# A new beginning for a talking-heads attention kernel: identity first, wider rows, a first chunk of nine tiles, six more score buffers, w_in later

## The chip, the cores and the metric

The kernel runs on one core of a Trainium2 chip. The metric is the device time of one execution in microseconds (us); "before" is the median of three runs. Engines: PE (matmul), DVE (vector), ACT (activation), POOL (GpSimd), SP (here only a queue that issues DMAs).

## The reference

```python
# q, k, v: (4 batches, 12 heads, 448 rows, 64), fp32
scores = scale * np.matmul(q, k.transpose(0, 1, 3, 2))
scores = np.einsum('bhij,hg->bgij', scores, w_pre)       # mixes the heads before the softmax
attn = exp(scores - max); attn = attn / (sum + 1e-09)
attn = np.einsum('bhij,hg->bgij', attn, w_post)          # and after it
x = np.matmul(attn, v)                                   # -> (4, 448, 768)
h = np.maximum(x @ w_in, 0.0)                            # 768 -> 1024
conv_out = sum over 3 taps of conv_w along the rows
out = (h * sigmoid(conv_out)) @ w_out                    # 1024 -> 768
```

The w_in, conv_w and w_out arrays are float64 and are turned to float32 in the kernel, piece by piece ("decode", five short steps on ACT, POOL and DVE).

## The kernel before

A **tile** is ten query rows of a batch with all twelve heads; its 120 lines (10 rows x 12 heads) and four lines of zeros lie on 124 partitions, so that one matmul by a block matrix of w_pre mixes the heads. A **chunk** is 12, 12, 12 or 9 tiles, four chunks to a batch, 16 in all (the table TILES). A chunk goes through these steps:

- `load_q`, `tr_q` / `load_k`, `tr_k`: queries of the chunk and keys of the batch, loaded and transposed. For the first chunks, `load_q0`, `load_k0` load rows as they lie and `tr_q0`, `tr_k0` transpose them on PE by an identity, `out_q0`, `out_k0` copy the result from PSUM. Later ones are transposed on DVE (L553, L569).
- `qk` (L588): scores of two heads at a time, four matmuls; `qk_out` (ACT L443, in chunks 0 and 1 every other one DVE L445) copies them to a buffer `st`, and `relayout` (L604, SP) moves that buffer into `mt`, one of two chunk buffers, where heads and rows share the partitions. There are three `st` buffers; for chunk 0 there is room for all twelve heads. A fourth score waits until the first relayout has landed.
- per pair of tiles: `premix` (L624; L617 where a tile is alone), `row_max` (DVE L629), `row_exp` (ACT L637), `sum_eps` (POOL), `sum_rec`, `post_w` (DVE L655), `postmix` (PE L668), `post_out` (ACT and DVE). The first premix of a chunk needs all twelve relayouts.
- per chunk: `av` (L709), `av_out`.

When a batch is through, `mm1` (L757) multiplies it by w_in, eight column blocks f, two in each chunk of the next batch; after the last chunk come the last batch's mm1 and the gated product with w_out (L851). w_in comes in 24 pieces (`dec_load`, L738), w_out in 24 more.

All instructions stand in an order found ahead of time by `plan`: each operation has a due time, in units of tiles, from a table of numbers P, a cost, and what it must wait for; a small model of the engines puts them in a row, and each engine runs its row in that order. Waits among engines are real semaphores, so an instruction whose input is late holds all that stand behind it on its engine.

The start is written out by hand: `load_weights` (POOL), `prepare` (zeros, the clearing of four partitions of both `mt` by POOL, L492, then the identity), twelve loads of keys and two of queries, `warm_up`, `emit_weights` (the block matrices of w_pre and w_post), and eight matmuls on zeros (`keep_busy`, L512).

Of the kernel before, what the change touches and what calls it, by code (L numbers as in the profile page):

```python
# [25 lines left out]
R, HR = 10, 5  # L26
TILES = (12, 12, 12, 9)
# [7 lines left out]
for _b in range(B):  # L35
    _i = 0
    for _t in TILES:
# [108 lines left out]

QUARTERS = [(hh, dh) for hh in range(2) for dh in range(2)]


def plan(P):  # L150
# [12 lines left out]
    for c in range(2):  # L163
        for g in range(2):
            n = -9 + g if c == 0 else P["q1p"] + .3 * g
            if c:
                add(n + P["q1l"], "SP", (.5, 10, .3), "load_q0", 1, g, after=[("load_q0", 1, g - 1)])
            add(n, "PE", .4, "tr_q0", c, g, after=[("load_q0", c, g)] + (
                [("tr_k0", 5)] + [("out_q0", 0, 0)] * g if c else []))
            add(n, ("DVE", "ACT")[g], .4, "out_q0", c, g, after=[("tr_q0", c, g), ("out_q0", c, g - 1)])  # L170
# [18 lines left out]

    for c in range(NCH):  # L190
        b, i0, T = CHUNKS[c]
        moved = [("relayout", c, h) for h in range(H)]
        for k, some in enumerate(PAIRS[c]):
# [4 lines left out]
            add(n + P["pm"], "PE", .78, "premix", *x,  # L198
                after=moved + free_m + ([("out_q0", 1, g) for g in range(2)] if at < 4 else []))
# [14 lines left out]
            for i in range(len(some)):  # L214
                add(n + 1 + P["po"] + .01 * i, "PE", .5, "postmix", *x, i, after=[("post_w", *x)] + (
# [65 lines left out]
    for i in range(N_PIECES):  # L281
# [6 lines left out]
        add(n - 4, "SP", (.45, 16, .85), "dec_load", i,  # L288
# [8 lines left out]
    for b in range(B):  # L297
        ready = [("av_out", 4 * b + 3, p) for p in (0, 3)] + [("dec_step", i, 4) for i in range(N_IN)]
        for f in range(FC):
            if b + 1 < B:  # L300
                n = BASE[4 * (b + 1) + f // 2] + P["m1"] + P["m1w"] * (f % 2)
                turn = [before["mm1", b, f]]
# [4 lines left out]
            for kk in range(KC):  # L307
                add(n + d * kk, "PE", .77, "mm1", b, f, kk, after=ready + turn + [("mm1", b, f, kk - 1)])
# [54 lines left out]
    for g in range(2):  # L363
        od.done["load_q0", 0, g] = 2.8 + 1.05 * g, "SP"
# [548 lines left out]
```

## Time and profile before

| | us |
|---|---|
| median of 3 runs | 710.15 (708.75 to 711.02) |
| profiled execution, device time | 710.14 |
| its span in the trace | 708.4 |
| PE busy | 663.8 (94% of the span) |
| DVE / ACT / POOL busy | 415.6 / 343.8 / 81.3 |
| DMA | 104.54 MB, mean 148 GB/s |

The span runs from the first to the last instruction on the core; the device time is 1.74 us longer. An engine's busy share is a mean over stages: the start, batch 0 without FFN work, batches 1 to 3 with it, and the end. PE's busy time comes from modelled ends of pipelined matmuls, and a matmul at the lower granted clock lasts twice as long and counts as busy all the same. A DMA share can go over 1, since packets in flight on an engine overlap.

### The profile page before, as it was taken

The numbers are of one execution on the slowest core, as the hardware profiler recorded it, in microseconds if no ns is written. First come the engines' busy times: TensorE is split into PE (matmuls) and PEld (weight loads), VectorE is DVE, ScalarE is ACT, GpSimd is POOL, SyncE is SP. The second block draws the span as 40 slices with busy tenths as digits, with TensorE's granted clock in tenths as the row PEclk, the third lists the DMA queues.
The fourth block names the chain that finished last, engine by engine and source line by source line (L and its number), as shares of the span: only waits on it lengthen the run. The fifth ranks groups of instructions, "written<-read, shape, count | busy, mean of one in ns | idle before, by whom it ended". The sixth has DMA issues, their size and how long they took to land.

```text
span 708.4 us, 23470 instructions
## 1 busy us (share of the span) xinstructions
PE 663.8 (94%) x9876; PEld 421.5 (59%) x9876; DVE 415.6 (59%) x976; ACT 343.8 (49%) x807; POOL 81.3 (11%) x185
## 2 busy tenths in 40 slices
PE   4687789798999999999999999999999999999997
PEld 3244434355474556555555646464565559999997
DVE  3365758776464647455665646454665499998000
ACT  1354637566464556656555755555554354434000
POOL 8010122222100001011001101101001000000000
PEclk7889979999999999999999999999999999999999
DMA  6577877878755467567746565542414344432111
GB/s 110 169 166 179 186 194 206 198 195 191 172 174 158 128 169 185 168 160 207 169 143 165 157 167 153 156 143 96 154 57 149 122 143 127 123 124 83 52 61 44
DMA packets 96005, 104.54 MB, mean 148 GB/s; under 512 B 40872, under 2 KB 84764, under 8 KB 95900
## 3 DMA queue, kind: packets, MB, share of 16 engines
q1 hardware_dynamic: 93997, 102.43, 53.8%
q8 instruction: 77, 1.26, 0.8%
q10 hardware_dynamic: 1807, 0.61, 0.4%
q14 instruction: 28, 0.23, 0.1%
q0 software_dynamic: 96, 0.01, 0.0%
HBM read 48.32 MB, written 15.99 MB: 91 GB/s over the span
## 4 chain that ended last, share of the span: by engine, by line
PE 75%; DMA 14%; DVE 3%; ACT 3%; POOL 2%; issue 1%; SPq 1%; ACTq 0%; DVEq 0%; POOLq 0%
PE h L757 20%; PE o L851 16%; PE s L588 12%; PE a L709 9%; PE t L668 9%; DMA mt<-st 9%; PE m L624 8%; DMA nq<-in_q_dram 2%; DMA raw<-in_moe_w_in_dram 2%; POOL mt L492 1%; DVE nm L629 1%; DMA raw<-in_moe_w_out_dram 1%; ACT st L443 1%; DMA wo<-w_out_s 1%; ACT e L637 1%
## 5 line engine op out<-in xcount | busy, mean ns | idle before, releaser
L757 PE MATMUL h<-x,wi 128*128 128x448 f32 x384 | 156.9, 552 | 0.9 <-DVE x L717 0.9
L588 PE MATMUL s<-mk,mq 64*64 64x448 f32 (+2 forms) x768 | 137.7, 572 | 9.6 <-ACT st L443 8.1
L637 ACT ACTIVATE e<-m,nm 124x448 f32<-124x448 f32 x180 | 114.7, 637 | 64.0 <-DVE nm L629 32.2
L443 ACT COPY st<-s 120x448 f32<-120x448 f32 (+1 forms) x180 | 92.4, 533 | 103.6 <-DMA mt<-st 42.6
L668 PEld LDWEIGHTS t<-wn,e 60*64 60x64 f32 x5760 | 104.0, 136 | 53.7 <-issue 33.2
L629 DVE TENSOR_REDUCE nm<-m 124x1 f32<-124x448 f32 x180 | 106.3, 614 | 50.3 <-PE m L624 50.1
L668 PE MATMUL t<-wn,e 60*64 60x60 f32 x5760 | 110.7, 221 | 9.3 <-DVE wn L655 4.3
L851 PE MATMUL o<-wo,g 128*128 128x384 f32 x672 | 117.4, 337 | 0.0
L851 PEld LDWEIGHTS o<-wo,g 128*128 128x128 f32 x672 | 116.9, 188 | 0.4 <-DVE g L836 0.2
L757 PEld LDWEIGHTS h<-x,wi 128*128 128x128 f32 x384 | 69.3, 190 | 75.5 <-issue 63.1
L624 PE MATMUL m<-mt,wpre 64*64 64x448 f32 (+1 forms) x704 | 102.1, 563 | 7.2 <-DMA mt<-st 3.9
L445 DVE COPY at<-t 128x480 f32<-128x480 f32 (+1 forms) x92 | 61.2, 665 | 55.3 <-PE t L668 55.1
L709 PEld LDWEIGHTS a<-at,v 128*64 128x64 f32 x1536 | 74.3, 137 | 20.8 <-issue 6.4
L709 PE MATMUL a<-at,v 128*64 128x120 f32 (+1 forms) x1536 | 83.6, 263 | 2.8 <-ACT at L443 1.6
L588 PEld LDWEIGHTS s<-mk,mq 64*64 64x64 f32 (+2 forms) x768 | 29.8, 130 | 65.0 <-issue 31.0
L643 POOL TENSOR_SCALAR sm<-sm 124x2 f32<-124x2 f32 (+1 forms) x92 | 20.9, 227 | 372.4 <-ACT e L637 341.4
L443 ACT COPY at<-t 128x480 f32<-128x480 f32 (+1 forms) x92 | 57.6, 626 | 3.5 <-PE t L668 3.5
L624 PEld LDWEIGHTS m<-mt,wpre 64*64 64x64 f32 (+1 forms) x704 | 27.8, 133 | 50.2 <-issue 32.1
L762 ACT ACTIVATE hs<-h 128x448 f32<-128x448 f32 x32 | 17.4, 542 | 54.9 <-PE h L757 54.9
L820 DVE SCALAR_TENSOR_TENSOR cv<-hpad,cws,cv 128x448 f32<-128x448 f32 x64 | 42.9, 681 | 0.2
L655 DVE TENSOR_SCALAR wn<-wpost,rs 124x60 f32<-124x60 f32 x180 | 38.0, 254 | 1.3
L637 ACT ACTIVATION_READ_ACCUMULATOR e<-m,nm 124x1 f32 x180 | 36.2, 201 | 0.0
(67 smaller groups left out, 374.0 us busy)
## 6 DMA issues: line engine op xcount, KB each, us to landing
mt<-st SPq DMA_DIRECT2D x144, 210.0 KB
nq<-in_q_dram SPq DMA_DIRECT2D x56, 168.0 KB
nk<-in_k_dram SPq DMA_DIRECT2D x72, 108.0 KB
mt<-st SPq DMA_DIRECT2D x48, 157.5 KB
h<-hs SPq DMA_DIRECT2D x32, 224.0 KB
hpad<-h SPq DMA_DIRECT2D x32, 224.0 KB
raw<-in_moe_w_in_dram SPq DMA_DIRECT2D x24, 256.0 KB
raw<-in_moe_w_out_dram SPq DMA_DIRECT2D x24, 256.0 KB
```

What stands on the lines that cost most here:

```text
L443: nc.scalar.copy(out=out, in_=in_)
L445: nc.vector.tensor_copy(out=out, in_=in_)
L588: nc.tensor.matmul(out=pqs[c, h - 1 + i][m:e], lhsT=qops[c][s, p, o + m:o + e], rhs=kops[b, p][s], start=True, stop=True)
L624: nc.tensor.matmul(out=pms[c, some[i]][64 * s:64 * s + 64], lhsT=wpre[rows, i], rhs=mt[rows, some[s]], start=True, stop=True)
L629: nc.vector.tensor_reduce(out=nm[0:PN], in_=pms[c, t][0:PN], axis=AX.X, op=ALU.max, negate=True)
L637: nc.scalar.activation(out=e[0:PN], in_=pms.pop((c, t))[0:PN], func=AF.Exp, bias=nm[0:PN], accum_out=sums[c, t // 2][0:PN, t % 2:t % 2 + 1])
L655: nc.vector.tensor_scalar(out=wns[c, k][0:PN, i], in0=wpost[0:PN], scalar1=rs[0:PN, i:i + 1], scalar2=None, op0=ALU.mult)
L668: nc.tensor.matmul(out=pts[c, k][s][64 * half:64 * half + 64, i, j], lhsT=e[rows, o:o + 64], rhs=wn[rows, i], start=True, stop=True)
L709: nc.tensor.matmul(out=pas[c][64 * hh:64 * hh + 64, p % 3, 0:n], lhsT=vts[b, p][:, hh, j, :], rhs=ats[c][:, j, 2 * p + hh, 0:n], start=(j ...
L757: nc.tensor.matmul(out=phs[b, f], lhsT=wi[:, kk, f * 128:(f + 1) * 128].bitcast(F32), rhs=xs[b][:, kk], start=(kk == 0), stop=(kk == KC - 1))
L820: nc.vector.scalar_tensor_tensor(out=cv, in0=hp[:, t:S + t], scalar=w, in1=cv, op0=ALU.mult, op1=ALU.add)
L851: nc.tensor.matmul(out=pos[r, o], lhsT=g, rhs=w, start=(f == 0 and j == 0), stop=(f == FC - 1 and j == 2))
```

## The change

- **Identity first.** `make_identity` is the first thing on POOL, ahead of `load_weights`. The four partitions of `mt` are cleared by two DMAs from a tile of zeros (`clear_mt`), and the operations of `emit_weights` that ran on DVE run on POOL.
- **Keys and queries in wider rows.** A partition of `load_k0` holds four consecutive rows of a head (1024 bytes, both heads in one DMA), one of `load_q0` two consecutive rows (512 bytes, before 256 for both); three query loads cover chunks 0 and 1, six DMAs the keys. Loads alternate between SP and ACT. The transposes become matmuls by the identity, eight to a pair of heads or to a group of four heads of queries, and the copies out put the rows back in order.
- **First chunk of 9 tiles** in batch 0 (9, 12, 12, 12), the other batches as before. In chunk 0 every other pair of heads uses two banks of the premix pool, so four banks take scores.
- **Six more score buffers** for chunks 1 to 3: `stx`, one tile of the x pool, whose slots and the three `st` are used in turn (`ring_slot`); from chunk 4 on there are three again.
- **w_in later**: its pieces are due every 3.76 tiles, not 1.6; an mm1 of batch 0 needs only the six pieces of its own column block. The whole table P has other numbers, and five matmuls on zeros stand in place of eight.

```diff
-TILES = (12, 12, 12, 9)
+TILES = [(9, 12, 12, 12)] + 3 * [(12, 12, 12, 9)]
...
+T0, T1 = TILES[0][:2]
+RH = R * (T0 + T1) // 2
+ST_X = 6
...
-    vl=0.707, nq=5.652, nqs=-4.258, tq=14.378, ahead=14.86, tk=2.029, tks=8.275, nk=7.972, dec=14.34, dwi=1.601,
+    nqs=-4.33, tq=14.316, ahead=17.24, tk=2.322, tks=0.913, nk=7.795, dec=14.624, dwi=3.76, dwo=5.594,
...
+def ring_slot(i):
+
+    if i < 4 * H:
+        s = (i - H) % (ST_X + 3)
+        return s - ST_X
+    return (i - 4 * H) % 3
...
-            free_st = [("relayout", *divmod(i - 3, H))] if i > 14 else []
+            free_st = [("relayout", *slot_of[i])] if i in slot_of else []
...
-                after=[("tr_q", c - 1, 3)] if c > 2 else [("tr_q0", 1, 1), ("relayout", 0, 11)])
+                after=[("tr_q", c - 1, 3)] if c > 2 else [("tr_q0", g) for g in range(3)])
...
-        ready = [("av_out", 4 * b + 3, p) for p in (0, 3)] + [("dec_step", i, 4) for i in range(N_IN)]
+        ready = [("av_out", 4 * b + 3, p) for p in (0, 3)] + [("dec_step", i, 4) for i in range(N_IN)] * (b > 0)
...
-                turn = [before["mm1", b, f]]
+                turn = [before["mm1", b, f]] + [("dec_step", i, 4) for i in range(f // 2 * KC, f // 2 * KC + KC)]
...
-            nc.vector.tensor_scalar(
+            nc.gpsimd.tensor_scalar(
...
-        nc.vector.tensor_copy(
+        nc.gpsimd.tensor_copy(
...
+    def identity():
+        nat["id"] = st_p.tile([128, 128], F32, tag="st", name="ident")
+        make_identity(nc, nat["id"])
...
-        for m in nat["mt"]:
-            nc.gpsimd.memset(m[0:4], 0.0)
...
+        nat["st"] = x_p.tile([128, ST_X, S], F32, tag="x", name="stx")
+
+    def clear_mt(i):
+        nc.sync.dma_start(out=nat["mt"][i][0:4],
+                          in_=nat["zero"].bitcast(F32)[0:4].rearrange("p (o j) -> p o j", o=1).to_broadcast([4, 12, S]))
...
+        eng.dma_start(out=nat["k0"][:, p].rearrange("j h c d -> j h (c d)"),
+                      in_=k[0, 2 * p:2 * p + 2].rearrange("h (j c) d -> j h (c d)", c=JC))
+
+    def load_q0(g, eng):
+        s = slice(4 * g, 4 * g + 4)
+        eng.dma_start(out=nat["q0"][:, s].rearrange("j n u d -> j n (u d)"),
+                      in_=q[0, s, 0:2 * RH].rearrange("n (j u) d -> j n (u d)", u=2))
...
         for c in range(JC):
-            nc.tensor.transpose(out=trs["k", p][:, 112 * c:112 * c + 112], in_=nat["k0"][:, p, c],
-                                identity=nat["id"][0:112, 0:112])
+            for hh in range(2):
+                nc.tensor.matmul(out=trs["k", p][64 * hh:64 * hh + 64, c], lhsT=nat["k0"][:, p, hh, c],
+                                 rhs=nat["id"][0:112, 0:112], start=True, stop=True)
...
+        pl, tag = (ps_m, "m") if c == 0 and p % 2 else (ps_q, "s")
         for i in range(2):
-            pqs[c, h - 1 + i] = ps_q.tile([128, S], F32, tag="s", name="s")
+            pqs[c, h - 1 + i] = pl.tile([128, S], F32, tag=tag, name="s")
...
-            st = st_p.tile([128, S], F32, tag="st", name="st")
+            s = ring_slot(c * H + h)
+            st = st_p.tile([128, S], F32, tag="st", name="st") if s >= 0 else nat["st"][:, s + ST_X]
...
     with tc.manual_schedule():
+        identity()
+        prepare()
+        for fn, i, eng in ((load_q0, 0, 0), (load_k0, 0, 1), (load_k0, 1, 0), (load_q0, 1, 1), (load_k0, 2, 0),
+                           (load_k0, 3, 1), (load_q0, 2, 0), (load_k0, 4, 1), (load_k0, 5, 0)):
+            fn(i, (nc.sync, nc.scalar)[eng])
         load_weights()
```

Three places in the order. First PE at the start (tq and tk are transposes of queries and keys, s the scores, m the premix). Before:

```order
L512 MATMUL idle<-zero 128x448 x8
L532 MATMUL tq_187<-ident,nq_147 128x120 x3
L532 MATMUL tq_191<-ident,nq_147 128x120 x3
L520 MATMUL tk_197<-ident,nk_146 128x112 x4
L520 MATMUL tk_205<-ident,nk_146 128x112 x4
L588 MATMUL s<-mk,mq 64x448 x2
L588 MATMUL s<-mk,mq 56x448 x2
L520 MATMUL tk_218<-ident,nk_146 128x112 x4
```

After:

```order
L533 MATMUL idle<-zero 128x448 x5
L555 MATMUL tq_180<-ident,nq_141 64x105 x8
L542 MATMUL tk_189<-ident,nk_140 64x112 x8
L542 MATMUL tk_202<-ident,nk_140 64x112 x8
L555 MATMUL tq_213<-ident,nq_141 64x105 x8
L614 MATMUL s<-mk,mq 64x448 x2
L614 MATMUL s<-mk,mq 26x448 x2
L542 MATMUL tk_232<-ident,nk_140 64x112 x8
L542 MATMUL tk_244<-ident,nk_140 64x112 x8
L542 MATMUL tk_256<-ident,nk_140 64x112 x8
L555 MATMUL tq_268<-ident,nq_141 64x105 x8
L542 MATMUL tk_279<-ident,nk_140 64x112 x8
```

After the first pair of heads, all other transposes now stand ahead of the second pair's scores; before they alternated, and the last of them (tq of chunk 1) stood behind the fifth pair.

Second SP's queue at the start (mt from st or stx are relayouts, nq loads of queries). Before:

```order
L506 DMA nq_147<-in_q_dram 120x6x64
L604 DMA mt<-st_223 10x12x448 x4
L506 DMA nq_147<-in_q_dram 120x6x64
L604 DMA mt<-st_223 10x12x448 x8
L604 DMA mt<-st 10x12x448 x3
L561 DMA nq<-in_q_dram 32x6x224 x4
```

After:

```order
L517 DMA mt<-zero 4x12x448 x2
L631 DMA mt<-st_241 10x9x448 x2
L586 DMA nq<-in_q_dram 32x6x224 x4
L631 DMA mt<-st_241 10x9x448 x10
L631 DMA mt<-stx 10x12x448 x3
L586 DMA nq<-in_q_dram 32x6x224
L631 DMA mt<-stx 10x12x448 x3
```

The four query loads of chunk 2 moved from behind chunk 0's relayouts and three of chunk 1's to behind chunk 0's first two; the ten others follow them.

Third SP's queue where the first pieces of w_in (raw) are loaded. Before, among the relayouts of chunk 2:

```order
L738 DMA raw<-in_moe_w_in_dram 128x512
L604 DMA mt<-st 10x12x448
L738 DMA raw<-in_moe_w_in_dram 128x512 x2
L604 DMA mt<-st 10x12x448
L561 DMA nq<-in_q_dram 32x6x224
```

After, among those of chunk 3:

```order
L765 DMA raw<-in_moe_w_in_dram 128x512
L631 DMA mt<-stx 10x12x448
L586 DMA nq<-in_q_dram 32x6x224
L631 DMA mt<-stx 10x12x448 x2
L572 DMA nk<-in_k_dram 32x864 x4
L631 DMA mt<-stx 10x12x448
L765 DMA raw<-in_moe_w_in_dram 128x512
```

The first piece comes a chunk later, and a second one only after eight other transfers. Up to the last relayout of chunk 4 the queue holds 19 pieces before and 9 after.

## Rows read from the trace of the kernel before

**Rows 1.** The page, part 2: 40 slices of the span, busy tenths, granted clock.

```profile
PE   4687789798999999999999999999999999999997
...
PEclk7889979999999999999999999999999999999999
```

**Rows 2.** Stretches: us, then busy us (instructions) of five engines, clock, DMA share, GB/s.

```profile
5.00:6.00 1.00, 0.00 (x0) 0.00 (x0) 0.00 (x0) 0.00 (x0) 1.00 (x1) 1.00 1.39 197
...
28.00:34.00 6.00, 3.65 (x27) 1.15 (x27) 1.25 (x2) 2.05 (x4) 0.00 (x0) 1.00 0.65 226
48.00:160.00 112.00, 95.75 (x1930) 50.33 (x1925) 78.66 (x205) 65.03 (x159) 21.52 (x41) 0.95 0.80 193
...
84.00:88.00 4.00, 1.32 (x65) 1.08 (x59) 3.06 (x9) 1.98 (x8) 1.06 (x2) 1.00 0.96 150
...
200.00:300.00 100.00, 100.00 (x1850) 57.38 (x1841) 56.37 (x136) 56.61 (x139) 6.45 (x21) 1.00 0.58 159
```

**Rows 3.** Timeline of the start: start us, us, engine, line, operation [idle before <-releaser].

```profile
3.38 9.08 POOL L492 MEMSET mt<- 4x5376 f32 x2
...
8.69 3.85 DVE L473 COPY wbd<-wraw 128x120 f32<-128x120 f32 x1 [1.71 <-DMA wraw<-in_w_post_dram]
...
12.42 0.27 POOL masks.py:197 MEMSET ident<- 128x128 f32 x1
...
13.11 1.46 PE L532 MATMUL tq<-ident,nq 120*128 120x120 f32 x6 [8.30 <-POOL warm L484]
...
16.69 1.76 PE L588 MATMUL s<-mk,mq 64*64 64x448 f32 x8 [0.63 <-DVE mq L445]
...
24.03 10.45 SPq L604 DMA_DIRECT2D mt<-st  x11
...
28.12 0.53 PE L532 MATMUL tq<-ident,nq 120*128 120x120 f32 x3 [1.20 <-DMA nq<-in_q_dram]
```

**Rows 4.** Timeline of PE: first premix (L624) of chunks 0 to 4, one FFN step.

```profile
36.45 1.77 PE L624 MATMUL m<-mt,wpre 64*64 64x448 f32 x8 [3.42 <-DMA mt<-st]
...
64.63 0.98 PE L624 MATMUL m<-mt,wpre 64*64 64x448 f32 x8 [0.56 <-DMA v<-in_v_dram]
...
102.50 0.98 PE L624 MATMUL m<-mt,wpre 64*64 64x448 f32 x8
...
129.68 0.61 PE L624 MATMUL m<-mt,wpre 64*64 64x448 f32 x4 [0.46 <-DMA mt<-st]
...
160.72 0.98 PE L624 MATMUL m<-mt,wpre 64*64 64x448 f32 x8
...
182.33 4.78 PE L757 MATMUL h<-x,wi 128*128 128x448 f32 x12
```

**Rows 5.** All instructions of the lone-tile premix, line 617: times in ns, starts in us.

```profile
L617 PEld LDWEIGHTS m<-mt,wpre x8: 182/184/187, 152.7 to 532.6; 124*124 124x124 f32 x8
```

**Rows 6.** Waits from 36 to 190 us: who waited for whom, us, times, longest.

```profile
ACT st L443 <- DMA mt<-st: 25.2, 27, 2.5
...
DVE st L445 <- DMA mt<-st: 9.7, 4, 5.4
```

**Rows 7.** Timeline of PE: the transposes of one pair of keys, and av.

```profile
18.37 1.01 PE L520 MATMUL tk<-ident,nk 112*128 112x112 f32 x4
...
61.30 1.86 PE L709 MATMUL a<-at,v 128*64 128x120 f32 x32 [0.87 <-ACT at L443]
```

**Rows 8.** DMA issues from 0 to 190 us: tile, queue, count, KB each.

```profile
mt<-st SPq DMA_DIRECT2D x60, 210.0 KB
raw<-in_moe_w_in_dram SPq DMA_DIRECT2D x24, 256.0 KB
nq<-in_q_dram SPq DMA_DIRECT2D x26, 168.0 KB
nk<-in_k_dram SPq DMA_DIRECT2D x34, 108.0 KB
v<-in_v_dram SPq DMA_DIRECT2D x22, 96.0 KB
```

More of the change, by code (lines that the diff above doesn't have):

```diff
@@ L36 @@
     _i = 0
-    for _t in TILES:
+    for _t in TILES[_b]:
         CHUNKS.append((_b, min(_i, S - R * _t), _t))
@@ L161, in plan @@
     place = {x: i for i, x in enumerate(tiles)}
[L163 to L170, printed above, removed]
+    for g in range(3):
+        add(-11 + g, "PE", .55, "tr_q0", g, after=[("load_q0", g)])
+        for c in range(2):
+            add(-10.8 + g + 2 * c, ("DVE", "ACT")[c], (.3, .35)[c], "out_q0", g, c, after=[("tr_q0", g)])
     for p in range(NP):
         n = P["k0a"] + P["k0d"] * p
-        add(n, "PE", .5, "tr_k0", p, after=[("load_k0", p), ("out_k0", p - 3)])
+        add(n, "PE", .6, "tr_k0", p, after=[("load_k0", p), ("out_k0", p - 3)])
         add(n, ("ACT", "DVE")[p % 2], .5, "out_k0", p, after=[("tr_k0", p)])
@@ L188, in plan @@
         before[y] = ("relu", *x[1:]) if x[0] == "mm1" else ("av_out", *x[1:])
+    slot_of, users = {}, {}
+    for i in range(H, NCH * H):
+        s = ring_slot(i)
+        if s in users:
+            slot_of[i] = divmod(users[s], H)
+        users[s] = i
     for c in range(NCH):
@@ L197, in plan @@
             free_m = [("row_exp", *tiles[j]) for j in range(max(0, at - 3), at - 3 + len(some)) if j >= 0]
-            add(n + P["pm"], "PE", .78, "premix", *x,
-                after=moved + free_m + ([("out_q0", 1, g) for g in range(2)] if at < 4 else []))
+            add(n + P["pm"], "PE", .753, "premix", *x,
+                after=moved + free_m + ([("qk_out", 0, h) for h in range(H)] if at < 4 else []))
             prev = pairs[number[x] - 1] if number[x] else None
@@ L214, in plan @@
             for i in range(len(some)):
-                add(n + 1 + P["po"] + .01 * i, "PE", .5, "postmix", *x, i, after=[("post_w", *x)] + (
+                add(n + 1 + P["po"] + .01 * i, "PE", .485, "postmix", *x, i, after=[("post_w", *x)] + (
                     [("post_out", *prev, s) for s in range(2)] if prev else []))
@@ L243, in plan @@
             turn = [before[x] for x in [("av", c, p)] if x in before]
-            add(n + P["av"], "PE", .82, "av", c, p, after=attn + [("load_v", b, p)] + turn + (
+            add(n + P["av"], "PE", .8 if T == 12 else .62, "av", c, p, after=attn + [("load_v", b, p)] + turn + (
                 [("av", c, p - 1)] if p % 3 else []))
@@ L361, in plan @@
         add(end + 14 + 4 * r + 6, "SP", (.4, 16, 1.0), "store", r, after=[("mm2_out", r, o) for o in range(2)])
-    for g in range(2):
-        od.done["load_q0", 0, g] = 2.8 + 1.05 * g, "SP"
+    for g in range(3):
+        od.done["load_q0", g] = 3.2 + 2.1 * g, "SP"
     for p in range(NP):
-        od.done["load_k0", p] = 5.15 + 1.28 * p, "SP"
-    order = od.run(dict(PE=5.2, ACT=3.9, DVE=5.0, POOL=7.4, SP=9.0), P["look"])
+        od.done["load_k0", p] = 3.8 + .7 * p + .7 * (p // 2), "SP"
+    order = od.run(dict(PE=4.0, ACT=4.2, DVE=2.0, POOL=9.0, SP=4.6), P["look"])
     return order, od
@@ L866, in tile_talking_heads_conv_glu @@
     emit = {f.__name__: f for f in (
[L867 removed]
+        tr_k0, out_k0, tr_q0, out_q0, load_k, tr_k, load_q, tr_q, qk, qk_out, relayout, premix, row_max,
         row_exp, sum_eps, sum_rec, post_w, postmix, post_out, zero_v, load_v1, load_v, av, av_out, load_cw, emit_cw,
@@ L872, in tile_talking_heads_conv_glu @@
     with tc.manual_schedule():
+        identity()
[3 more added lines that the diff above has]
+            fn(i, (nc.sync, nc.scalar)[eng])
         load_weights()
-        prepare()
-        loads = [(load_q0, 0, 0), (load_q0, 0, 1)] + [(load_k0, p) for p in range(NP)]
-        for i, (fn, *a) in enumerate(loads):
-            fn(*a, nc.scalar if i in (1, 3) else nc.sync)
         warm_up()
@@ L880, in tile_talking_heads_conv_glu @@
         keep_busy(P["busy0"])
+        for i in range(2):
+            clear_mt(i)
         for name, *a in plan(P)[0]:
```

75 lines of the change are left out of this document (35 added, 40 removed).

## The prediction

> **What bounds the kernel now.** I read the page's slices first: PE is busy 94% of the span, but not evenly. The slices up to about 190 us carry sevens and eights and a lowered clock, all later ones nines [rows 1]. So the end is set by PE from 200 us on (100.00 of 100.00 us busy) and by something else before [rows 2]. What can be won lies in the first batch.
>
> Then the start in the timeline. POOL clears a corner of the two score buffers for 9.08 us and only then builds the identity; the first transposes wait 8.30 us for POOL and begin at 13.11, though loads already ran at 197 GB/s at 5 us [rows 2, 3]. Scores follow at 16.69, and SP issues relayouts back to back, eleven in 10.45 us from 24.03. Among them stands a load whose transposes hold PE until 28.12, with the last pair of chunk 0 behind them [rows 3]. The first premix of chunk 0 runs at 36.45 [rows 4].
>
> Then I laid the chunk starts beside each other: first premix of chunks 0 to 4 at 36.45, 64.63, 102.50, 129.68 and 160.72 [rows 4]. What would PE alone need? The lone-tile premix that closes each batch runs four times from 152.7 to 532.6, so a batch takes (532.6 - 152.7)/3 = 126.6 us in the saturated part [rows 5]. It holds eight steps of the FFN's first product, one (f) of six matmuls each for the batch before; one of these, twelve records, took 4.78 us [rows 4], so eight are 38.2 us. Attention alone is 126.6 - 38.2 = 88.4 us for 45 tiles, 1.96 us a tile. Batch 0, with no FFN in it, took 160.72 - 36.45 = 124.3 us: **35.9 us more than PE needs**, behind a start of 36.4 us. The largest waits there are evictions of scores for a free staging buffer, that is, for an earlier relayout to land: ACT 25.2 us, DVE 9.7 us [rows 6]. Three buffers in flight pace the whole batch.
>
> From the first premix of chunk 4 to the end it is 708.4 - 160.7 = 547.7 us, nearly all of it PE. So the time is **547.7 + (start of chunk 4) + (what the change makes worse later) + 1.74**; the last is the profiled execution's 710.14 less its span of 708.4, and that execution stands at the median of 710.15.
>
> **The start: first premix at 27 instead of 36.45.** The identity is now POOL's first work (two operations of under 0.3 us [rows 3]), so transposes wait for data only. Loads: three of 210 KB for queries and six of 224 KB for keys, 2.02 MB (KB are 1024 bytes). Before, the 256-byte rows moved at 197 GB/s [rows 2]; at that rate, from 2 us, the last key lands at 12.2. No row shows 512- and 1024-byte rows from HBM at this point; the near row on the fast side is 226 GB/s for relayouts [rows 2], which gives 10.9. I take 12. The Trainium skill (DMA: Bandwidth & Descriptors, Specifications) puts the line rate at rows of 512 B and more, which by its HBM limit would end the loads nearer 8 us and bring the first premix near 23 (an estimate); no row here shows that.
>
> PE has all six key transposes and three query groups ahead of pairs 1 to 5 of chunk 0, so these wait for the last key. The transposes are now matmuls by the identity: eight of 128x64 by 112 columns per pair of heads. The row nearest in shape is the av product, 32 records (two sets of eight) in 1.86 us, so 0.9 us a set against 1.01 for the old four [rows 7]. Nine sets are 8 us and lie beside the loads; after the last load one set is left, 0.9 us. Then a pair, 1.76 us at the low clock [rows 3]; for it and its eviction I count 1.7 at the full clock: SP's third relayout can go at about 14.6. At 10.45/11 = 0.95 us each [rows 3] the last of the ten goes nine later, near 23. Before, the last relayout of chunk 0, the eighth of the eleven, was issued near 31.5 and the premix ran at 36.45, 5 us later. That gives 28; with the loads of chunk 2's queries now ahead of the ten and chunk 0 a quarter smaller per relayout I take **27**, 24 if the loads come early, 30 if the transposes run at the low clock (then 2 us a set).
>
> Costed at nothing, with the cover: five small operations move from DVE to POOL; on DVE one of them took 3.85 us [rows 3], so at worst 19 us behind weights that had landed by 8.7. Only the first premix and post_w need them, 27 and 29; if the cover failed it would be about 3 us. The corner is cleared by two DMAs ahead of the relayouts (0.17 MB). Four banks in place of two for chunk 0 let two pairs run ahead; SP is slower than both. SP's four query loads for chunk 2 now wait for the third query group on PE, ten relayouts behind them; that group runs at about 11 us, before the tenth could go. The copies out of the transposes are strided now; they lie under the loads. The six buffers take one of two x tiles, first needed again when chunk 4's av is copied out, long after chunk 3's last relayout.
>
> **Chunks 0 to 3.** With six more buffers, nine relayouts can be in flight until chunk 4. Then either PE or the DMA engines set the start of chunk 4.
> - PE: 27 + 88.4 = 115.4.
> - DMA: up to the last relayout of chunk 4 SP's order holds 48 relayouts of 210 KB and 12 of three quarters of that, 20 query loads, 24 key loads, 12 value loads with a third of one each per pair (six), and now 9 pieces of w_in instead of 19 [rows 8]. With the first loads and the clears that is 24.3 MB (before: 27.9 MB). Less the first 2.0, 22.3 MB remain from 12 us on. Before moved 193 GB/s over 48 to 160 us [rows 2]: 22.3/0.193 = 115.5 us, chunk 4 at **127.5**. At 226 GB/s it would be 111, under PE's 115.4.
>
> I take 127.5: the 193 GB/s came with slots as the brake, so it is no hard ceiling, but the engines were 0.80 busy over it, and relayouts alone ran at 226 GB/s with 0.65 [rows 2], so there is not much above. That is 33 us of the 35.9 + 9.5 = 45 us that are there to be won. Chunk 0 with nine tiles lets the first premix come earlier but gives chunk 1 three tiles (6 us) less to hide under; it is inside this sum, since both bounds count all 45 tiles.
>
> **w_in later.** Fifteen pieces now load after chunk 4 begins, beside the FFN of batch 0; each FFN step waits only for its own six pieces. In the planned order the twelfth piece is decoded well before the third step and the twenty-fourth before the seventh, so no PE instruction stands directly behind one. What it costs is traffic: 15 x 0.26 = 3.9 MB over some 100 us on top of 159 GB/s [rows 2], 198 GB/s, near what the engines moved when PE idled in batch 0. I take 3 us, between 0 and 8.
>
> Sum: 547.7 + 127.5 + 3 = 678.2 of span, **680 us**, 4.2% faster.
>
> **The rivals.**
> - *PE alone bounds batch 0.* Nine slots keep the engines full, the rate goes over 22.3/(115.4 - 12), 216 GB/s, and chunk 4 begins at 116: 547.7 + 116 + 0 to 3 + 1.7 = 665 to 668. For it: 226 GB/s at a share of 0.65 shows that relayouts leave a third of the engines idle, so other loads fit beside them. Taken as ten full engines of sixteen, relayouts put 1.23 MB on each of the ten and the rest 0.63 MB; 1.86 MB at 22.6 GB/s are 82 us, done at 94, under PE. Against it: v and q come in short rows. The Trainium skill (DMA: Bandwidth & Descriptors, Why a DMA increments its semaphore by 16 and not by 1) says just this, that a DMA takes the largest count up to 16 dividing both sides' slowest dimension, here 10; the share of 0.65 agrees.
> - *Only the start is won.* The queue's order, not the slots, paces batch 0, and its excess of 35.9 us stays: chunk 4 at 27 + 124.3 = 151.3, time 700.7. For it: SP is one queue in order, and PE waited also for evictions and for DVE.
> - *Slower.* More relayouts in flight get in each other's way and the mean rate falls. Break-even is 22.3 MB in 160.7 - 12 us, 150 GB/s; the stretch 84 to 88 us ran at just that with the engines at 0.96 [rows 2]. At 145 GB/s chunk 4 begins at 166 and the time is 715. Against it: that stretch is one of 4 us, and the 112 us around it moved 193 at 0.80.
>
> **How the numbers follow.** Forecast 0.60 (668 to 692), PE-bound 0.17 (665 to 668), start only 0.17 (around 701), slower 0.06 (715). The range runs from 662 (first premix at 24, PE-bound, nothing lost later: 547.7 + 112.4 + 1.7) to 701; it leaves out the slower case, the upper half of the start-only one and a little below. A measurement of this kernel tells 0.3%, 2 us, from no change: faster 0.93, within 0.02, slower 0.05.
>
> **What would show it.** The first transposes at 4 to 5 us; the last key's near 12; chunk 0's first premix near 27; chunks 1 to 4 near 45, 68, 92 and 127; evictions waiting for relayouts far under the 25.2 us; 193 GB/s or more from 30 to 130 us; PE without gaps from chunk 4 on. I am wrong if chunk 4 begins after 150 (slots were not the brake), if the stretch behind chunk 4 grows beyond 556 us (w_in), or if the first premix comes after 32.

## The result and the profile after

The changed kernel takes **687.54 us** (median of 4, 683.89 to 690.48) against 709.67 for the kernel before on the same chip: ratio 0.9684, 95% interval 0.9624 to 0.9744, 3.2% faster. The forecast was 680, the range 662 to 701. The profiled execution is the 690.48, the slowest of the four; its span is 688.7.

The page's slices and its chain of waits, which answer to [rows 1]:

```profile
PE 659.7 (96%) x9981; PEld 425.9 (62%) x9981; DVE 412.0 (60%) x974; ACT 343.2 (50%) x808; POOL 75.1 (11%) x186
...
PE   8899969799989999999999999999999999999997
...
PEclk9889988989999999999999999999999999999999
...
PE 85%; DMA 6%; ACT 3%; DVE 3%; issue 2%; SPq 1%; POOL 0%; ACTq 0%; DVEq 0%
```

Over the first eight slices together (138 us) PE is busier than before, though not in each of them, and four still show a granted clock under nine tenths: batch 0 is better, not saturated.

The first premix of chunks 0 to 4 (timeline of PE; line 651 is line 624 of before; answers to [rows 4]) and the lone-tile premix that closes the chunk of nine tiles (answers to [rows 5]; in batch 0 it now closes chunk 0):

```profile
35.38 1.83 PE L651 MATMUL m<-mt,wpre 64*64 64x448 f32 x8
...
52.64 0.98 PE L651 MATMUL m<-mt,wpre 64*64 64x448 f32 x8
...
73.62 0.98 PE L651 MATMUL m<-mt,wpre 64*64 64x448 f32 x8
...
104.20 2.13 PE L651 MATMUL m<-mt,wpre 64*64 64x448 f32 x8
...
142.83 0.98 PE L651 MATMUL m<-mt,wpre 64*64 64x448 f32 x8
...
L644 PEld LDWEIGHTS m<-mt,wpre x8: 183/184/186, 45.8 to 512.7; 124*124 124x124 f32 x8
```

From these starts, chunk by chunk, beside what PE needs at the prediction's 1.96 us a tile:

| chunk of batch 0 | before: tiles, us | PE needs | after: tiles, us | PE needs |
|---|---|---|---|---|
| 0 | 12, 28.2 | 23.5 | 9, 17.3 | 17.6 |
| 1 | 12, 37.9 | 23.5 | 12, 21.0 | 23.5 |
| 2 | 12, 27.2 | 23.5 | 12, 30.6 | 23.5 |
| 3 | 9, 31.0 | 17.6 | 12, 38.6 | 23.5 |
| start of chunk 4 | 160.72 | | 142.83 | |

The first premix is only 1.1 us earlier than before, yet chunk 4 begins 17.9 us earlier. Chunks 0 and 1 now take no longer than the prediction's figure for PE; the excess that is left, 107.5 - 88.2 = 19 us of the former 36, lies in chunks 2 and 3. From chunk 4 to the end it is 688.7 - 142.8 = 545.9 us, before 547.7.

Waits from 36 to 190 us (who waited for whom, us, times, longest), and stretches of the changed kernel, with the columns of [rows 2]:

```profile
ACT st L460 <- DMA mt<-st: 5.9, 6, 2.2
DVE mk L578 <- DMA nk<-in_k_dram: 4.0, 3, 2.1
DVE stx L462 <- DMA mt<-st: 2.0, 1, 2.0
```
```profile
12.00:143.00 131.00, 115.10 (x2284) 66.79 (x2284) 82.57 (x203) 72.70 (x179) 15.58 (x44) 0.90 0.76 184
...
52.00:73.00 21.00, 19.91 (x484) 11.41 (x486) 14.62 (x41) 16.31 (x44) 1.59 (x7) 1.00 0.68 179
73.00:104.00 31.00, 25.46 (x632) 17.57 (x630) 20.91 (x51) 16.74 (x42) 3.02 (x8) 0.89 0.81 186
104.00:143.00 39.00, 33.63 (x699) 22.34 (x696) 26.33 (x67) 21.45 (x53) 7.81 (x16) 0.87 0.85 206
...
126.00:134.00 8.00, 5.21 (x153) 3.14 (x153) 6.96 (x22) 4.96 (x12) 2.23 (x5) 1.00 0.98 207
```

The waits of evictions for a free score buffer (`st`, `stx`) fell from 34.9 us [rows 6] to 7.9. In chunk 1 PE is busy 19.91 of 21 us while the DMA engines idle a third of the time; in chunk 3 the engines are busy 0.85 of it, 0.98 at 126 to 134 us, with DVE busy 6.96 of these 8 us (the decoding of w_in is part of it), and PE has gaps.

The start, stretches and timeline (answer to [rows 2, 3]; PEld is PE's weight loader, which works beside PE):

```profile
4.00:6.00 2.00, 0.77 (x10) 0.81 (x12) 0.00 (x0) 0.40 (x2) 0.00 (x0) 1.00 1.13 257
6.00:8.00 2.00, 2.00 (x27) 2.00 (x26) 0.35 (x1) 0.37 (x1) 0.00 (x0) 1.00 1.15 244
8.00:10.00 2.00, 2.00 (x39) 1.87 (x38) 0.75 (x1) 1.02 (x2) 1.01 (x4) 1.00 1.13 219
10.00:12.00 2.00, 2.00 (x16) 0.56 (x16) 0.80 (x3) 0.61 (x2) 1.76 (x5) 1.00 0.51 102
...
15.00:24.00 9.00, 9.00 (x54) 2.05 (x50) 3.69 (x6) 2.58 (x6) 0.00 (x0) 1.00 0.83 173
...
29.00:39.00 10.00, 8.72 (x44) 3.12 (x47) 3.18 (x6) 2.62 (x6) 0.00 (x0) 0.50 0.73 204
```
```profile
0.80 0.20 POOL masks.py:197 MEMSET ident<- 128x128 f32 x1 [0.29 <-POOLq L927]
...
5.23 1.67 PE L555 MATMUL tq<-ident,nq 105*64 105x105 f32 x16 [1.54 <-DMA nq<-in_q_dram]
...
8.42 0.99 ACT L460 COPY mk<-tk 128x448 f32<-128x448 f32 x1 [1.12 <-PE tk L542]
...
14.70 0.94 PE L542 MATMUL tk<-ident,nk 112*64 112x112 f32 x16
...
15.57 0.19 PEld L614 LDWEIGHTS s<-mk,mq 64*64 64x64 f32 x4
...
16.47 0.13 PEld L614 LDWEIGHTS s<-mk,mq 64*26 64x26 f32 x4 [0.70 <-issue]
...
17.34 0.19 PEld L614 LDWEIGHTS s<-mk,mq 64*64 64x64 f32 x4 [0.74 <-issue]
...
17.44 0.53 ACT L460 COPY st<-s 90x448 f32<-90x448 f32 x1 [1.97 <-PE s L614]
...
17.99 8.72 SPq L631 DMA_DIRECT2D mt<-st  x10
...
24.55 0.93 DVE L594 STREAM_TRANSPOSE mq<-nq 128x384 f32<-128x384 f32 x1 [1.15 <-PE s L614]
...
28.77 1.89 PE L614 MATMUL s<-mk,mq 64*64 64x448 f32 x8 [0.63 <-ACT stx L460]
```

Transposes begin at 5.23 instead of 13.11, and the loads are over soon after 10 us. But from 6 to 25 us PE has next to no idle time: the last keys' transposes come at 14.70 for want of PE, not of data. A score pair of a nine-tile chunk has two column blocks, 64 and 26 wide, and the weights of the second are loaded 0.90 us after those of the first, those of the next pair 0.87 us later: 1.77 us a pair at the full clock, so the last scores of chunk 0 end near 24.5. And before the first premix PE's order holds five pairs of chunk 1, of which those from 28.77 on take 1.89 us each at the low clock (0.50 from 29 to 39 us), each waiting for an eviction.

### The profile page after: what moved, and what is told of

The parts are those of the page before. It is cut to its first block, busy times and chain, and to the rows that moved or that the text cites. A ratio compares the mean times of both kernels' runs of the same rounds, so it can differ in the third digit from the quotient of the medians.

```text
span 688.7 us, 23692 instructions
## 1 busy us (share of the span) xinstructions
PE 659.7 (96%) x9981; PEld 425.9 (62%) x9981; DVE 412.0 (60%) x974; ACT 343.2 (50%) x808; POOL 75.1 (11%) x186
## 4 chain that ended last, share of the span: by engine, by line
PE 85%; DMA 6%; ACT 3%; DVE 3%; issue 2%; SPq 1%; POOL 0%; ACTq 0%; DVEq 0%
PE h L784 21%; PE o L878 17%; PE s L614 14%; PE t L695 11%; PE a L736 10%; PE m L651 10%; DMA nq<-in_q_dram 2%; ACT e L664 1%; DMA nk<-in_k_dram 1%; DMA v<-in_v_dram 1%; DMA raw<-in_moe_w_in_dram 1%; PE tk L542 1%; ACT at L460 1%; DVE nm L656 1%; DVE mq L594 1%
## 5 line engine op out<-in xcount | busy, mean ns | idle before, releaser
L784 PE MATMUL h<-x,wi 128*128 128x448 f32 x384 | 159.1, 555 | 0.0
L695 PEld LDWEIGHTS t<-wn,e 60*64 60x64 f32 x5760 | 106.5, 137 | 47.8 <-issue 28.6
L614 PE MATMUL s<-mk,mq 64*64 64x448 f32 (+2 forms) x768 | 126.5, 577 | 7.4 <-ACT st L460 2.6
L460 ACT COPY st<-s 120x448 f32<-120x448 f32 (+1 forms) x161 | 82.1, 536 | 79.4 <-PE s L614 32.6
L651 PE MATMUL m<-mt,wpre 64*64 64x448 f32 (+1 forms) x704 | 96.5, 568 | 6.4 <-ACT e L664 3.0
L736 PEld LDWEIGHTS a<-at,v 128*64 128x64 f32 x1536 | 75.9, 139 | 22.9 <-issue 6.4
L736 PE MATMUL a<-at,v 128*64 128x120 f32 (+1 forms) x1536 | 86.3, 266 | 2.9 <-DVE at L462 0.9
L614 PEld LDWEIGHTS s<-mk,mq 64*64 64x64 f32 (+2 forms) x768 | 28.0, 131 | 63.3 <-issue 32.7
L651 PEld LDWEIGHTS m<-mt,wpre 64*64 64x64 f32 (+1 forms) x704 | 25.3, 134 | 44.6 <-issue 30.3
L789 ACT ACTIVATE hs<-h 128x448 f32<-128x448 f32 x32 | 17.3, 542 | 47.5 <-PE h L784 34.5
```

What stands on the lines that cost most here:

```text
L460: nc.scalar.copy(out=out, in_=in_)
L614: nc.tensor.matmul(out=pqs[c, h - 1 + i][m:e], lhsT=qops[c][s, p, o + m:o + e], rhs=kops[b, p][s], start=True, stop=True)
L651: nc.tensor.matmul(out=pms[c, some[i]][64 * s:64 * s + 64], lhsT=wpre[rows, i], rhs=mt[rows, some[s]], start=True, stop=True)
L695: nc.tensor.matmul(out=pts[c, k][s][64 * half:64 * half + 64, i, j], lhsT=e[rows, o:o + 64], rhs=wn[rows, i], start=True, stop=True)
L736: nc.tensor.matmul(out=pas[c][64 * hh:64 * hh + 64, p % 3, 0:n], lhsT=vts[b, p][:, hh, j, :], rhs=ats[c][:, j, 2 * p + hh, 0:n], start=(j ...
L784: nc.tensor.matmul(out=phs[b, f], lhsT=wi[:, kk, f * 128:(f + 1) * 128].bitcast(F32), rhs=xs[b][:, kk], start=(kk == 0), stop=(kk == KC - 1))
```

## The experiments

The comparisons are ratios to the kernel before. First premix, start of chunk 4 and the stretch behind it, read in each trace as above:

| kernel | median us | ratio, 95% | first premix | chunk 4 | chunk 4 to end of span |
|---|---|---|---|---|---|
| before | | | 36.45 | 160.72 | 547.7 |
| changed | 687.54 | 0.9684 (0.9624 to 0.9744) | 35.38 | 142.83 | 545.9 |
| slots3 | 696.55 | 0.9813 (0.9740 to 0.9886) | 39.45 | 151.57 | 543.3 |
| win_early | 700.54 | 0.9856 (0.9790 to 0.9922) | 35.65 | 145.16 | 557.7 |
| keys_spread | 690.67 | 0.9726 (0.9667 to 0.9784) | 33.90 | 150.88 | 542.2 |
| tiles12 | 692.25 | 0.9744 (0.9696 to 0.9792) | 36.99 | 142.84 | 547.9 |
| b_ident | 707.61 | 0.9953 (0.9924 to 0.9981) | 33.19 | 158.47 | 547.3 |
| b_winlate | 709.28 | 0.9978 (0.9960 to 0.9996) | 36.62 | 155.28 | 552.4 |
| b_slots | 715.28 | 1.0060 (1.0028 to 1.0092) | 36.24 | 157.90 | 552.3 |
| b_slots_win | 709.93 | 0.9966 (0.9935 to 0.9996) | 40.42 | 158.31 | 549.9 |
| pad0 | 686.36 | 0.9655 (0.9602 to 0.9708) | 35.57 | 138.34 | 544.0 |
| pad0_dve | 682.33 | 0.9606 (0.9569 to 0.9643) | 30.43 | 135.02 | 544.7 |
| padall | 675.81 | 0.9508 (0.9483 to 0.9534) | 34.66 | 140.88 | 534.6 |
| padall_dve | 670.16 | 0.9429 (0.9393 to 0.9464) | 30.05 | 134.20 | 531.8 |

The last three columns come from one profiled execution each. Those of the changed kernel, win_early and keys_spread lie 2.9, 4.1 and 4.2 us above their medians, those of b_slots, pad0 and padall_dve 3.4, 2.3 and 2.4 below: a difference of two or three us in these columns can be chance.

**The buffers (slots3): the changed kernel with three buffers in its unchanged order.**

```diff
-            s = ring_slot(c * H + h)
-            st = st_p.tile([128, S], F32, tag="st", name="st") if s >= 0 else nat["st"][:, s + ST_X]
+            st = st_p.tile([128, S], F32, tag="st", name="st")
```

> After, in the same order of instructions, but chunks 1 to 3 have the three staging buffers only. If the six buffers are what shortens batch 0, its excess over PE's 88 us (19 us in after, 36 in before) goes back to about 36 and the time to about 704 us, with evictions waiting for relayouts for 20 us and more. If the start and the order alone bring the gain, it stays under 692.

Measured 696.55, 9 us over the changed kernel and between the two figures expected; the first premix is 4.1 us later and chunk 4 8.7. The excess over PE's 88.2 us is 151.57 - 39.45 - 88.2 = 24 us, not the 36 of before. In the waits of slots3, 36 to 190 us, the evictions' are back:

```profile
ACT st L460 <- DMA mt<-st: 15.5, 11, 2.6
...
DVE st L462 <- DMA mt<-st: 2.6, 1, 2.6
```

18.1 us of waits against 7.9. The buffers are worth 9 us of the 22 inside the changed kernel, in an order that was planned for nine of them, and 4 of these already before the first premix, which the prediction had not counted there.

**w_in (win_early): the changed kernel with the old pace of w_in**, in a newly planned order. Of the long line of table P only the numbers that differ are shown, here and below.

```diff
-dec=14.624, dwi=3.76
+dec=14.34, dwi=1.601
```

> After, but the pieces of w_in are due as early as before (every 1.6 tiles). If DMA traffic sets the start of chunk 4, ten pieces more ahead of it (2.6 MB at 0.19) put it 10 to 14 us later and the time at 695 to 701. Rival: the engines move only 170 GB/s up to there and have room; the time stays within 3 us of 687.5.

Measured 700.54, 13 us over the changed kernel, but chunk 4 is only 2.3 us later; the other 12 lie behind it (557.7 us against 545.9). So the time fell where expected and the mechanism did not hold. The planner moved the whole order: not ten pieces more but four stood ahead of chunk 4 (15 against 11 issued by its first premix), with four query loads fewer. This is the price of a plan, not only of the early bytes; how much is which was not separated.

**Batch 1's keys (keys_spread).** The changed table also bunches the key loads of batch 1 (tks 8.275 to 0.913), which the prediction passed over. Undone, again in a newly planned order:

```diff
-tk=2.322, tks=0.913, nk=7.795
+tk=2.029, tks=8.275, nk=7.972
```

> After, but the keys of the next batch are due over the batch as in before, not in one burst. Theory: the burst of 24 key loads from 83 to 111 us holds DVE at the key transpose (2.05 us) and the queries of chunk 4 (6.1 us to land), which makes the gap of PE from 92.6 to 104; spread out it saves 4 to 8 us. Rival: the same bytes only move to another place, within 2 us of 687.5.

Measured 690.67: the interval of its ratio covers the changed kernel's. Chunk 4 begins 8 us later and the rest is 3.7 us shorter. Spreading the loads brought none of the 4 to 8 us expected; that theory fell.

**The parts alone, on the kernel before.** The identity first, the corners by DMA and the weights on POOL:

```diff
+        nat["id"] = st_p.tile([128, 128], F32, tag="st", name="ident")
+        make_identity(nc, nat["id"])
...
-            nc.gpsimd.memset(m[0:4], 0.0)
...
+            nc.sync.dma_start(out=nat["mt"][i][0:4], in_=nat["zero"].bitcast(F32)[0:4].rearrange(
```

> Before, with the first part of the change alone: identity first on POOL, the corners of mt cleared by DMA, weights made on POOL. Transposes at 4 to 5 us, first premix near 28 and not 36.45. If the start is simply ahead of everything, the 8 us reach the end: about 702. Rival: chunk 1 and 2 wait for relayouts out of three buffers and take the gain back: 707 to 710.

w_in later alone, with the waits of its steps on their own pieces:

```diff
-dec=14.34, dwi=1.601
+dec=14.624, dwi=3.76
...
-                turn = [before["mm1", b, f]]
+                turn = [before["mm1", b, f]] + [("dec_step", i, 4) for i in range(f // 2 * KC, f // 2 * KC + KC)]
```

> Before, with w_in later alone (a piece every 3.76 tiles, each FFN step waiting for its own six). If traffic ahead of chunk 4 costs what the run with w_in early showed in after (13 us), the time falls by 8 to 13 us to about 699. Rival: with three buffers the buffers are the brake, and it stays within 3 us of 709.6.

The six buffers alone:

```diff
-            free_st = [("relayout", *divmod(i - 3, H))] if i > 14 else []
+            free_st = [("relayout", *slot_of[i])] if i in slot_of else []
...
+        nat["st"] = x_p.tile([128, ST_X, S], F32, tag="x", name="stx")
...
+            st = st_p.tile([128, S], F32, tag="st", name="st") if s >= 0 else nat["st"][:, s + ST_X]
```

> The kernel before with the six additional score buffers in batch 0 alone (same tables, same start, w_in early, first chunk of 12 tiles). Theory (buffers are the main brake of batch 0, whatever the start): ACT's 25.2 us of waits for relayouts between 36 and 190 us falls under 10, and the time falls by the 9 us that the buffers were worth within the changed kernel, to about 700. Rival (without w_in moved away the queue is full anyway and the buffers only move the wait to the transfers): within 3 us of 710.

And both edits together (b_slots_win):

> The kernel before with the six additional score buffers and w_in later, without the new start, the wider rows and the short first chunk. Theory (the parts help each other: w_in's early bytes cost only where the buffers let the queue run ahead): more than the sum of the two alone, 10 or more below the kernel before with the buffers alone giving 9 and w_in alone 1: 690 to 696. Rival (the parts only add): 699. If it comes out near 687, the new start is worth nothing.

Alone, none is worth much: 707.61, 709.28, 715.28, and 709.93 for the two together, against 710 to 711 for the kernel before. In b_ident and b_winlate the rivals held; b_ident's first premix came at 33.19, not near 28, and still 2.2 us ahead of the changed kernel's. b_slots came out 0.6% slower, some 4 us, which neither its theory nor its rival had; of the rival, the mechanism is seen, a wait that moved to the transfers. Its waits, 36 to 190 us, then its chain of waits between 120 and 200 us (start us, us, what):

```profile
ACT st L461 <- DMA mt<-st: 15.3, 14, 1.9
```
```profile
127.51 9.02 DMA mt<-st
...
143.30 6.55 DMA raw<-in_moe_w_in_dram
...
152.46 7.12 DMA raw<-in_moe_w_in_dram
...
159.64 8.63 DMA mt<-st
```

The evictions' waits fell from 34.9 to 15.3 us, as they should, and the lone-tile premix of batch 0 came at 144.45, 8 us earlier than before [rows 5]. But chunk 4 began only 2.8 us earlier: between the two, the chain runs through transfers, w_in among them. And the stretch behind it grew by 4.6 us. The gain of one part is taken by the next wait. With w_in moved too, my theory (690 to 696) and the sum of the parts (699) were both wrong: 709.93. What tiles12 has beyond b_slots_win is the new start, the wider rows, four banks for chunk 0's scores and the new numbers of the planner's table, and it is 17.7 us faster. Of these only the first, the identity with the corners and the weights, was run alone, worth about 3 us (ratio 0.9953); how the rest divides was not tried and stays open. Counted this way it is most of the 22 us.

**The first chunk of nine tiles (tiles12): the changed kernel with twelve again.**

```diff
-TILES = [(9, 12, 12, 12)] + 3 * [(12, 12, 12, 9)]
+TILES = 4 * [(12, 12, 12, 9)]
```

> The changed kernel with the first batch cut into 12, 12, 12 and 9 tiles as in the kernel before; everything else of the change stays. The score pairs of chunk 0 are then two equal blocks and cost about 0.98 us instead of 1.77, but its relayouts carry a third more bytes before the first premix. Theory (the nine-tile first chunk is worth little, because its pairs cost 10.6 us where twelve-tile pairs cost 5.9): first premix at 34 to 37, and the end within 5 us of the changed kernel's 687.5. Rival (the short first chunk is what brings the first premix forward, since less has to be moved ahead of it): first premix near 40 and the time near 693 to 700.

Measured 692.25. The first premix is 1.6 us later, chunk 4 at the same time to 0.01 us. The theory holds: the short first chunk does little, 4.7 us by the medians. That this is because its pairs cost more than those of twelve tiles is argued here; the next runs bear on it.

**The slow pairs (pad0): chunk 0's scores computed for 128 rows**, so that both column blocks are 64 wide; the relayout takes the 90 rows as before.

```diff
-        n = R * CHUNKS[c][2]
+        n = R * CHUNKS[c][2] if c else 128
...
-                e = min(m + 64, n)
+                e = m + 64 if c == 0 else min(m + 64, n)
```

> After, but chunk 0's scores are made for 128 query rows (64 + 64) and 90 of them copied out, so that the second pair of matmuls in each pair of heads has 64 columns of weights and not 26. Theory: 26 columns don't run beside 64, so a pair takes 1.77 us; padded it takes about 0.98 at the full clock, six pairs save 4 to 5 us, the first premix comes at 31 and not 35.4, the time falls by about 4 us from 687.5. Rival: the first premix stands behind chunk 1's pairs and the queue of relayouts anyway; it moves by 1 us or less and the time stays within 2 us.

Timeline of pad0:

```profile
15.90 5.21 PE L614 MATMUL s<-mk,mq 64*64 64x448 f32 x48
...
24.03 0.86 DVE L594 STREAM_TRANSPOSE mq<-nq 128x384 f32<-128x384 f32 x1 [3.95 <-DMA nq<-in_q_dram]
...
26.58 1.75 PE L614 MATMUL s<-mk,mq 64*64 64x448 f32 x6 [3.88 <-DVE stx L462]
...
35.57 1.83 PE L651 MATMUL m<-mt,wpre 64*64 64x448 f32 x8
```

Six pairs (five of chunk 0, one of chunk 1) in 5.21 us, 0.87 each instead of 1.77: more columns in half the time. But the first premix stands where it stood. DVE waits 3.95 us for a query load of chunk 2, and the eviction of chunk 1 stands behind that transpose in DVE's order, so PE waits 3.88 us for the eviction. The same order is in the changed kernel (24.55 in its timeline), where the slow pairs end only then.

**That order removed (pad0_dve):**

```diff
+        late = [("tr_q", 2, 0), ("tr_q", 2, 3)]
+        order = [x for x in order if x not in late]
+        at = order.index(("qk_out", 1, 5)) + 1
+        order[at:at] = late
```

> pad0 with one change of order: on DVE the two query transposes of chunk 2 stand behind chunk 1's first three evictions and no longer ahead of them. In pad0 PE waited 3.9 us there while the queries of chunk 2 landed. Theory: this wait is what held the first premix at 35.6; it comes at 31 to 32, chunk 1 near 49, the time falls by 3 to 4 us to 683. Rival: chunk 1's start is set by its relayouts in SP's queue; the first premix moves, chunk 1 and the end don't.

The transposes now stand behind the third of DVE's evictions of chunk 1. First premix at 30.43, chunk 4 at 135.02, 682.33: with the slow pairs gone, this wait was what still held the first premix at 35.57. The order alone, with the slow pairs left in, was not run.

**Every nine-tile chunk for 128 rows (padall):** the edit of pad0 with `T == 9` in place of `c == 0`; in the later batches the eviction copies all 128 rows and the relayout takes the 90 that are wanted.

> After, with every chunk of nine tiles padded to 128 query rows for its scores, not only chunk 0. In the saturated part a pair of such a chunk takes 1.6 to 1.8 us of PE, one of a twelve-tile chunk 0.9 to 1.0. If PE bounds there, three chunks of six pairs give 18 x 0.7 = 13 us: about 673. Rival: evictions and buffers pace the scores of these chunks, the time falls by 4 us or less from pad0's 686.4.

Measured 675.81. The stretch behind chunk 4 is 11.3 us shorter than in the changed kernel. The three later batches have 18 such pairs, and 18 x (1.77 - 0.87) is 16 us at most. That the later pairs are slow as well is read from the changed kernel, all 24 narrow pairs and all pairs of 64 and 56 (groups by shape: count, busy us, mean ns, idle before):

```profile
L614 PEld LDWEIGHTS s<-mk,mq 64*56 64x56 f32 x288 | 14.8, 132 | 0.0
...
L614 PEld LDWEIGHTS s<-mk,mq 64*26 64x26 f32 x96 | 3.1, 99 | 16.9 <-issue 16.9
```

The weight loader stands idle for 16.9 us ahead of the narrow blocks, 24 x 0.70, and not at all ahead of those 56 wide.

**Both (padall_dve), with the order of pad0_dve** (behind DVE's third eviction of chunk 1, not its last):

> The changed kernel with both remedies: every nine-tile chunk's score pair computed for 128 query rows (two equal blocks of 64 columns) and the two query transposes' work for chunk 2 on DVE moved behind chunk 1's last eviction. Theory (the wide second block cost PE time in every batch, the DVE order cost the start): the two gains lie in different stretches, so they add: 675.8 of the first remedy alone less the 4 that the second gave to the other version, 672, with the first premix near 30.5 instead of 34.7 and chunk 4 near 137. Rival (the start's gain is eaten later by the transfers, since the same bytes have to pass before chunk 4): chunk 4 stays near 141 and the time near 676.

Measured 670.16, a ratio of 0.9429 (0.9393 to 0.9464): 5.7% under the kernel before, and the fastest of all. The gains add. Its first premix and, from its chain of waits, what stands just before; then PE's line on the pages of padall and of this kernel:

```profile
30.05 1.56 PE L652 MATMUL m<-mt,wpre 64*64 64x448 f32 x8 [2.28 <-issue]
```
```profile
24.36 4.38 DMA mt<-st
```
```profile
PE 642.8 (95%) x9981; PEld 427.4 (63%) x9981; DVE 411.1 (61%) x974; ACT 343.1 (51%) x808; POOL 75.2 (11%) x186
```
```profile
PE 636.5 (96%) x9981; PEld 424.9 (64%) x9981; DVE 412.0 (62%) x974; ACT 343.6 (52%) x808; POOL 75.2 (11%) x186
```

PE has the same 9981 instructions in all three. In padall, whose execution had the changed kernel's mean clock of 0.977, it is busy 16.9 us less, where 24 pairs at 0.9 us would be 21.6. The 23.2 us less of padall_dve are not all the pairs': its clock was 0.989.

## Why the prediction was right, and where its terms were off

The direction and the range held: 687.5 in 662 to 701. The mechanism held in part: batch 0 was what could be won, the rest stayed PE's, and nine buffers took away most of the evictions' waits. But they are worth 9 us of the 22, and what set the start of chunk 4 was not what the sum has. The sum missed by 10.5 us of span (678.2 against 688.7): +15.3 at chunk 4, -4.8 behind it; that the two have opposite signs is luck.

- **First premix at 27: it came at 35.38**, past the 32 that I had named as a sign of being wrong. Transposes began at 5.23, near what I said. The step that failed is the one that takes the last load as the start's pace ("after the last load one set is left") and then SP as the only pace. PE was full from 6 us: sets of transposes and six pairs at 1.77, 10.6 us, which I had let run under SP's relayouts, keep it until 24.5. Then five pairs of chunk 1 stand in its order ahead of the premix, the second of them behind DVE's transposes for chunk 2 and the last three at the low clock. pad0 and pad0_dve show both causes: 35.57 with the pairs mended, 30.43 with the order mended as well. I had taken the premix to follow the last relayout of its chunk and had not read what else PE's order holds in between. The 3 us from 30.43 to 27 are SP's: its third relayout went out at 17.37 in pad0_dve (17.99 in the changed kernel) and not at 14.6, the following ones came at the pace I had taken (8.72 us for ten), and the premix then does wait for the last of them, 2.3 us.
- **Loads.** I took 2.02 MB by 12 us, between rates of 197 and 226 GB/s. The stretches from 4 to 8 us moved 257 and 244, and from 10 us on the rate falls to 102: the wider rows came faster than either bound. PE was behind, so it is likely that this won nothing; the wider rows alone were not run. The Trainium skill (DMA: Bandwidth & Descriptors, Specifications) has the line rate for rows of 512 B and more; I had worked out an end of the loads near 8 us and a first premix near 23 from it, as an estimate. The loads ended between that and my 12; the premix at 23 fell, because of PE.
- **DMA bound, 22.3 MB at 193 GB/s, chunk 4 at 127.5: it began at 142.83.** In the term's own units there are two parts. From 12 to 143 us the rate was 184 GB/s, which alone gives 12 + 22.3/0.184 = 133.2. And 184 x 131 us is 24.1 MB: until then 63 relayouts, 24 query loads and 11 pieces of w_in had been issued, I had counted 60, 20 and 9, which is 1.86 MB or 10 us at this rate. Together 143. But bytes over their mean rate give the time whatever the cause, and the engines were busy 0.76 of it; this does not show that they set the start of chunk 4. The chain of waits of the changed kernel, 12 to 200 us, says where transfers held it up:

```profile
78.75 2.93 DMA raw<-in_moe_w_in_dram
...
83.41 7.79 DMA nk<-in_k_dram
...
93.21 6.10 DMA nq<-in_q_dram
...
120.31 3.36 DMA raw<-in_moe_w_in_dram
...
137.08 3.47 PE a L736 x32
```

In chunk 2 these are 16.8 of 30.6 us. In chunk 3, which has 15 of the 19 us of excess, it is one piece of w_in. From 124 us to chunk 4 the chain names no transfer, only DVE, ACT and PE one behind the other, with PE's clock at 0.57 from 134 to 142; the last relayout of chunk 4 had gone out at 130.52, 12 us before its premix.
- **The form of that step was wrong as well.** I took the larger of two totals, PE's 88 us and the engines' 115. The stretches show that the bounds take turns: PE in chunk 1 with the engines at 0.68, transfers in chunk 2, and in chunk 3 PE, busy 33.63 of 39 us at a mean clock of 0.87, in turn with DVE and ACT. So a late start is not hidden by a DMA bound: pad0_dve's premix leads pad0's by 5.1 us, chunk 4 by 3.3 (138.34 to 135.02), and the medians differ by 4.0.
- **w_in later, +3: the stretch behind chunk 4 became 1.8 us shorter**, outside my 0 to 8. The cost that the term meant is seen on the kernel before: in b_winlate chunk 4 begins 5.4 us earlier and the stretch behind it is 4.7 longer. In win_early, where the old pace got a new order, the stretch is 12 us longer, which I had only looked for ahead of chunk 4.
- **Costed at nothing:** the weights on POOL held (its last operation on them, wpost, ends at 13.2, long before 35). The strided copies take 0.99 us for a pair of keys; what they cost the start was not tried.
- **Rivals.** PE alone (665 to 668) is refuted by the 19 us of excess that remain in batch 0. "Only the start is won" fails the other way round: the first premix gained 1 us and chunk 4 nearly 18. The slower case needed 150 GB/s and the stretch held 184; b_slots, 0.6% slower than before, is the only run on that side, and what makes its later stretch longer was not tested.

## What to carry to other kernels

Where two resources take turns as the bound, sum the larger of the two over stages, and do not take the larger of two sums (such a sum by stages was not made here). Before putting a time on the first result of a stage, read every instruction that stands ahead of it on its engine, and on the engines that empty its banks, and time each by its own shape: half as many columns are not half the time. And the worth of one edit, alone, on a kernel whose next wait is close says little about its worth in company: here buffers gave nothing or a loss alone and 9 us together with the rest.

## What the runs showed of the hardware

- **Two column blocks of one score pair overlap at 64 and 64, not at 64 and 26.** The first take 0.87 us a pair, the others 1.77, both at the full clock, with the second block's weights loaded 0.70 us after PE's weight loader fell idle. The 120-row pairs, 64 and 56, overlap too (0.96 us for the pair at 122.71 us of the changed kernel, at the full clock). Between 26 and 56 nothing was run, and why the narrow block waits the records don't say.
- **Strided copies out of PSUM cost nearly double here:** 0.99 us for 128 x 448 with the rows put back in order, 0.53 us for ACT's plain copies of 90 or 120 x 448 in the same trace.
- **Slower executions had a lower granted clock.** The changed kernel's four: 690.48 at a mean of 0.977, 689.91 at 0.985, 685.18 at 1.000, 683.89 at 0.994. With four runs that is a trend, not a law. Inside one run, two stretches in which PE waited were followed by stretches at or near the lower of the clock's two levels (1.2 of 2.4 GHz). PE waits 2.4 us before 96.13, and the clock is 0.55 over 96 to 107; it is busy 5.21 of 8 us at 126 to 134, and the clock is 0.57 over the next 8:

```profile
96.00:107.00 11.00, 7.76 (x127) 4.54 (x131) 5.90 (x14) 3.42 (x8) 1.07 (x2) 0.55 0.93 201
...
134.00:142.00 8.00, 6.58 (x95) 5.04 (x97) 2.87 (x5) 1.41 (x3) 1.25 (x3) 0.57 0.84 222
```
